# Mixed-head attention with two feed-forward layers: v in seven DMAs by key, weight DMAs on two queues, another listed order

## The chip, the cores and the metric

One core of a Trainium2 chip runs the whole program. The metric is the device time of one execution in microseconds. The kernel before has a median of 1281.13 us in 3 runs (1278.77 to 1286.63). The profiled execution took 1281.71 us, with a span of 1280.0 us from its first to its last instruction.

## The reference, cut to what matters

Four batches of 12 heads, 448 positions, head size 64, all float32. The scores of all heads are mixed by a 12x12 matrix before the softmax, and the attention weights by another one after it:

```python
scores = scale * np.matmul(q, k.transpose(0, 1, 3, 2))
scores = np.einsum('bhij,hg->bgij', scores, w_pre)
attn = exp(scores - max); attn = attn / (sum + 1e-09)
attn = np.einsum('bhij,hg->bgij', attn, w_post)
x = np.matmul(attn, v)                       # then to [1792 tokens, 768]
x = (1 / (1 + exp(-(x @ w_gate))) * (x @ w_val)) @ w_out     # d_ff 1536
h = x @ w_in; out = (h * (1 / (1 + exp(-1.702 * h)))) @ w_out2   # d_ff 2048
```

## The kernel before

**Stages.** Attention comes first, about the first 388 us of the span, and the two feed-forward layers fill the rest. In attention, queries go in 16 units (4 a batch, 120 queries or 88 in the last). For each unit TensorE forms the scores of the six head pairs (`qk`, L343), the scores are copied to SBUF (`sc`), and the SP queue's DMAs rearrange them (`relayout`, L362, tile `gt`), so that one partition holds one query of one head. The units are cut into 92 groups. For each group, in order: two relayouts, `premix` (TensorE, L371), `rowmax` (VectorE, L377), `expo` (ScalarE, L383), `norm` in three steps (ScalarE L391, VectorE L393, GpSimd L396, which makes the tile `w`), `postmix` (TensorE, L418), and copies to the tile `at` (L306). When a unit's groups are done, `av` (TensorE, L439) multiplies `at` with the tile `vt` of its batch, the result is copied to `xo`, and `store` (L456) writes it to DRAM.

**Buffers that couple these.** There are five `gt` buffers, one `at`, one `vt`, one `pf` and two `pc`. So v of a batch can be loaded only after the last `av` of the batch before it, and the first `av` of its own batch waits for it.

**v before.** `load_v` (L325, the DMA at L329) fills `vt`. Key 7m+g of a head stands in partition m + 64*(g // 4) and column g % 4. The kernel before loads it in 8 DMAs a batch, each for three heads and for g = 0 to 3 or g = 4 to 6. A run of 4 or 3 neighbouring keys is one packet of 1024 or 768 bytes. Each DMA writes 64 partitions.

**Weights during attention.** `prepare` (L928) takes 28 blocks of the first layer's weights through attention: a DMA brings a block of 384 KB into `pf` (L938, packets of 1024 bytes), ScalarE (L896, L897) and VectorE (L899, L900, L902) change its number format into `pc`, and a DMA writes 192 KB to the DRAM tensor `kept` (L904). All of these DMAs are issued by SP.

**The order.** Each such step is a numbered piece, given to `work.add` with its needs, the buffers that it takes and gives, the engines that may run it and durations that were used to plan. `PLAN` is a written list of all pieces in the order in which they are emitted. A token is the piece's number in base 36, a letter for the engine where it is not the first one allowed (S ScalarE, V VectorE, P GpSimd, Y SP), and after a colon the PSUM banks. `order()` (L45) reads the list and chooses nothing. Every engine and every DMA queue works through its own pieces in this order, and a piece whose semaphore is not there yet holds up all behind it on that engine or queue.

Of the kernel before, what the change touches and what calls it, by code (L numbers as in the profile page):

```python
# [9 lines left out]
F32 = mybir.dt.float32  # L10
# [69 lines left out]
32 33 3a:34 3b 4q 4r 3p 3r 3d 5dV 2s:62 2tS 3c 3e 40:57 2uS 5cS 34 35:60 41 3f 3s 3g 42 3h 43 44 4d:34 4e 4f  # L80
4g 3i:21 3jS 4h 36V 37S 4i 3kV 45 4j 82:57 88:36 89V 8b:21 46 8aS 83S 3t 8e:40 8cV 84V 8gV 85:63 87V 1gl 86S
8fS 4k 47 8h:52 1gm 4s 8dS 4t 4u 48:76 4l:04 4mS 8jS 49V 4aS 4nS 4v dt:3 duV 5n 5o 3u 60 61 6d 6e 6q 6r 73
3v:17 3wS 1gn 3xS 5p:02 5q 62:64 8iS 5s 4w:1 4x 6f:75 dz 6g 74 5r 5t 5u 6i 5v 7g 7h 8k 8l 1go 4y 50:0 51 6h 52
6j 63 65 dv 1g5 6s:27 64 6t 66 67 68 6k 5w 6v 4zS 6u 5x:56 5yS 75:34 5zV 76 69 6a:12 6bV 8x 8y 6l 6m 1gq e0
az:56 78 6w 77 b1S 53V 6x 6y 7i:73 6n:16 7j 79 7l 8m:04 6oV 6cS 9a 9b b0S 7k 7m 7n 6z 6pV 7a 9n 70:25 7o 9o
71S 72S ds 7p 7b 7c b8:71 ef 8n 8o b9V b5:36 b2:25 1gr b7V b3S b4S a0 1gp 8p e1:7 1gs e2S 7q:06 baV 8q en e3
8r e7 1gt 7d:21 7rS 1gu 7eS 9c:54 7fV 7sS 8z:70 b6V 9d 9f 9p:26 9q 90 9s 9e 9g 9r 1gw a1 91 9t e4:1 e5V dw:3
dxS 7t:5 7u 7v 7wS be:42 bgS 8s 54P bb:76 bdV 1gx dy 1gy qe eh:5 eiS 92 ej 93 ad ae 8t e6 1g6 1gz 1h0 ep:2 eqS
er 7x:6 e8 9u 9h 9i 9j qm 7y eg 7z 80S qf 94 bcS 1h2 a2:35 a3 bfS a5 eo 8u:01 af:62 ag e9:7 qg:4 a4 8vS 8wS a6
qhS 9v 1gv eaV ai ec:3 edV qo:0 eb a7 a8 ee ah bh bi aj ak 9k:15 9lS ek:6 9mV ev:72 ewS ey:31 exS f0S qi bu bv  # L90
c7 elV f1:54 f2S a9 qpV qj:7 al am 1h1 qkS 9w c8 ezS f3V qq ql es:2 etS aa:15 abS eu 1h3 1h4 an:40 aoS 9x:37
95 96 fa:21 9yS 9zS ck cl qu em acV apS f7:46 f9S fbS f8S 1h5 1h6 fcS f4:35 f6V bj:70 f5V bk bm bw:62 bx bl cx
bz 97:54 bn 98V 99S cy 1h8 c9:31 ca cc cm:70 cb bo aq:4 ar as by cn au:5 c0 av aw cd 1g7 cp atS c1 81P ce bp
bq cz:36 cf co c2 1h9 1ha cq fd cr cs 1hb 1hc c3 axS d0 cg fe fq fr g3 g4 gg br:21 bsS d2 ff:47 fg 1h7 ct d1
d3 btV gh fh gt 1he ch:05 ciV cjS fi cu:23 cvV i0:61 i9:40 iaV cwS fj ayP d4 gu ibS i6:53 i7V d5 fk fl i3:27
h6 h7 if:40 i8S i1S ic:35 idV ieV i4S i2S ihS fs:62 ft i5S g5:10 fv gi:73 1hd qv g6 igS fu fw fx c4:45 fy d6
d7:62 c5V c6S d8V d9S gv:54 gw 1hf gx gy fm qn da:2 db dc de:6 df gz g7 1hg g8 g9 ga ii h0 ij iv gj gl gk gm
1hh 1hi gn gb dg fn:54 foV gc iw j8 j9 jl jm ddV fz h8:10 h9 qr:7 hb h1 h2 fpS 1hk qsV 1g8 g0:34 dhS ik:52 il
ha in qt g1S g2S hj hc go gp gd:61 im io kx:34 geV hk kyS l9:05 laV lbV 1hl h3:72 h4S kzV hl hm hn ho hp l6:63
hq hd ip l7V l8S l3:05 l5S l4S 1hm 1hn he hf 1ho gfS lc:74 l0:36 ldV jy l2S h5S jz gq:50 l1S jn:16 1hj kb grV  # L100
ix:72 iy iq gsS hg:35 hhV ir j0 leS hiS ja:04 iz j1 j2 j3 jb jo jq jc 1hq kc ra lf hr:5 jd lg ls je hs ht huS
hv:3 hw hx 1hp hyV 1hr jp 1hs k0:72 is:04 lt m5 k1 jr k3 jf itV kd:53 m6 1g9 k2 mi iuV k4 139 j4 ke nu:16 nvV
k5 js nx:70 nwS jg jh k6 kg 1ht j5:24 kf rc:6 mj kh ki nyV nzS 1hu qw:1 ri rdS j6S jt qxV kj qy ji:53 jjV 1hw
jkS r2 j7S lh:70 ju li lk lj ll lu:21 lv lx kk lw jv:35 rb o6:47 ly o8S qz:0 k7 re r0S r1 mk:26 ml jwS r3 mn
# [54 lines left out]
def attention(tc, q, k, v, w_pre, w_post, xd, after):  # L159
# [7 lines left out]
    nc = tc.nc  # L167
    B, H, S, D = q.shape
# [37 lines left out]
    nu = len(units) // B  # L206
# [1573 lines left out]
```

## Time and profile before

| what | value |
|---|---|
| median of 3 runs | 1281.13 us |
| profiled execution, its span | 1281.71 us, 1280.0 us |
| PE, DVE, ACT, POOL busy | 97%, 78%, 64%, 5% of the span |
| PE instructions | 12770 matmuls, 12770 weight loads |
| DMA packets | 215855, of them 60028 under 512 bytes |
| HBM read, written | 160.18 MB, 55.97 MB |

Busy shares are averages over the two stages, which differ: attention has 8,000 of the matmuls in about 388 us, most of them small. The queue SPq is SP's; its DMAs have a row when they are issued, and the time that a row shows is that of the issue. PE's "issue" as a releaser is idle time in which PE waited for nothing that the profile shows. The granted clock of PE is 1.00 for 2.4 GHz and 0.50 for 1.2 GHz. DMA share is the mean busy share of the 16 DMA engines; as packets of several queues overlap, it can pass 1.

### The profile page before, as it was taken

How to read it: one execution, taken by the hardware profiler on the slowest of the kernel's cores; microseconds unless marked ns; L12 is line 12 of the kernel's file. 1: busy time of each engine (PE TensorE's matmuls, PEld its weight loads, DVE VectorE, ACT ScalarE, POOL GpSimd, SP SyncE). 2: the span in 40 equal slices, each digit the busy share in tenths (PEclk: the TensorE clock that was granted, in tenths of full speed). 3: DMA queues.
4: the chain of work that ended last, by engine and by line, in shares of the span. 5: the costliest groups of instructions: out<-in, count | busy, mean ns of one | idle time of the engine just before them, and what ended most of it. 6: DMA issues, size and time to landing. Idle time of an engine off the chain costs nothing.

```text
span 1280.0 us, 33240 instructions
## 1 busy us (share of the span) xinstructions
PE 1243.6 (97%) x12770; PEld 1112.2 (87%) x12770; DVE 998.1 (78%) x2134; ACT 822.6 (64%) x1976; POOL 58.5 (5%) x139
## 2 busy tenths in 40 slices
PE   7999998899989999999999999999999999999998
PEld 4677676687779899989999999999999989999998
DVE  5687787888877999898799888779756795565763
ACT  3788787888764776776567666556655555565432
POOL 3111111111100000000000000000000000000000
PEclk9999999999999999999999999999999999999999
DMA  6777878778667654589875545885526872125643
GB/s 163 219 203 232 217 217 239 202 236 232 224 217 240 211 180 149 166 294 330 306 270 185 165 157 195 275 287 193 178 77 195 277 256 81 54 68 159 211 147 124
DMA packets 215855, 256.88 MB, mean 201 GB/s; under 512 B 60028, under 2 KB 202160, under 8 KB 215696
## 3 DMA queue, kind: packets, MB, share of 16 engines
q1 hardware_dynamic: 208992, 248.97, 61.6%
q0 software_dynamic: 1488, 4.51, 1.2%
q8 instruction: 101, 1.65, 0.5%
q10 hardware_dynamic: 5216, 1.26, 0.5%
q14 instruction: 58, 0.48, 0.1%
HBM read 160.18 MB, written 55.97 MB: 169 GB/s over the span
## 4 chain that ended last, share of the span: by engine, by line
PE 49%; DVE 7%; DMA 6%; ACT 2%; issue 2%; SPq 0%; DVEq 0%; ACTq 0%
PE pq L1161 27%; PE po L1648 16%; PE py L1106 6%; DMA ws<-in_moe_w_in_dram 3%; DMA sb<-xy 2%; DVE w L1028 1%; DVE xy L1143 1%; DVE s L1299 1%; DVE wc L900 1%; ACT ws L897 1%; ACT xy L1142 1%; DVE wc L902 1%; DVE s L1170 1%; DMA xy<-kept 0%; ACT w L1022 0%
## 5 line engine op out<-in xcount | busy, mean ns | idle before, releaser
L1161 PE MATMUL pq<-xy,w 128*128 128x448 f32 x2394 | 482.3, 362 | 1.8 <-ACT s L1210 0.9
L1161 PEld LDWEIGHTS pq<-xy,w 128*128 128x128 f32 x2394 | 447.7, 187 | 35.8 <-ACT s L1210 2.4
L1648 PE MATMUL po<-wf,xy 128*128 128x384 f32 x1176 | 206.9, 337 | 2.6 <-ACT xy L1094 1.6
L1648 PEld LDWEIGHTS po<-wf,xy 128*128 128x128 f32 x1176 | 206.1, 188 | 3.3 <-ACT xy L1094 1.9
L1106 PE MATMUL py<-xy,w 128*128 128x448 f32 x864 | 173.7, 362 | 1.4 <-DVE xy L1092 1.4
L1106 PEld LDWEIGHTS py<-xy,w 128*128 128x128 f32 x864 | 161.9, 187 | 12.9 <-DVE xy L1092 2.1
L383 ACT ACTIVATE ex<-bank,st 128x448 f32<-128x448 f32 x184 | 116.0, 638 | 23.9 <-DVE st L377 23.7
L418 PEld LDWEIGHTS bank<-w,ex 60*64 60x64 f32 (+1 forms) x5152 | 100.2, 134 | 34.9 <-issue 26.6
L1142 ACT CAST xy<-xy 128x384 fp32r<-128x384 f32 (+2 forms) x212 | 89.3, 457 | 58.2 <-DVE xy L1299 55.1
L377 DVE TENSOR_REDUCE st<-bank 128x1 f32<-128x448 f32 x184 | 106.4, 614 | 21.2 <-PE bank L371 20.9
L418 PE MATMUL bank<-w,ex 60*64 60x60 f32 (+2 forms) x5152 | 104.1, 220 | 9.8 <-issue 8.8
L1143 DVE TENSOR_TENSOR xy<-xy 128x384 fp32r<-128x384 f32 (+2 forms) x212 | 95.5, 483 | 23.1 <-ACT xy L1142 22.7
L1299 DVE TENSOR_TENSOR xy<-xy 128x384 f32<-128x384 f32 (+2 forms) x184 | 90.7, 510 | 14.8 <-DMA xy<-kept 7.2
L371 PE MATMUL bank<-gt,wpre 64*64 64x448 f32 (+2 forms) x736 | 95.1, 552 | 1.8 <-DMA gt<-sc 1.2
L1022 ACT CAST w<-xy 128x384 fp32r<-128x384 f32 x110 | 55.2, 510 | 51.8 <-DVE xy L1299 30.9
L439 PEld LDWEIGHTS bank<-at,vt 128*64 128x64 f32 x1536 | 73.9, 137 | 14.0 <-ACT at L306 5.4
L896 ACT ACTIVATE wc<-ws 128x384 f32<-128x384 f32 x108 | 59.8, 554 | 35.2 <-DMA ws<-in_moe_w_in_dram 24.8
L439 PE MATMUL bank<-at,vt 128*64 128x120 f32 (+1 forms) x1536 | 78.7, 261 | 2.4 <-issue 1.3
L1028 DVE TENSOR_TENSOR w<-wt,w 128x384 fp32r<-128x384 f32 x108 | 59.1, 552 | 26.9 <-ACT w L1022 26.9
L343 PE MATMUL bank<-kq 64*120 64x448 f32 (+1 forms) x576 | 73.9, 393 | 2.8 <-issue 1.8
L306 ACT COPY sc<-bank 120x448 f32<-120x448 f32 (+1 forms) x121 | 59.4, 546 | 19.0 <-DMA nat<-in_q_dram 9.0
L1170 DVE TENSOR_TENSOR s<-s,pq 128x448 f32<-128x448 f32 x80 | 49.2, 616 | 28.5 <-PE pq L1161 28.4
(98 smaller groups left out, 1524.0 us busy)
## 6 DMA issues: line engine op xcount, KB each, us to landing
gt<-sc SPq DMA_DIRECT2D x160, 210.0 KB
wf<-sb SPq DMA_DIRECT2D x64, 384.0 KB
xy<-kept SPq DMA_DIRECT2D x60, 384.0 KB
ws<-in_moe_w_out_dram SPq DMA_DIRECT2D x56, 384.0 KB
kept<-wc SPq DMA_DIRECT2D x108, 192.0 KB
ws<-kept SPq DMA_DIRECT2D x46, 384.0 KB
sb<-xy SPq DMA_DIRECT2D x32, 384.0 KB
ws<-in_moe_w_in_dram SPq DMA_DIRECT2D x32, 384.0 KB
```

The lines of the kernel that those rows point to most:

```text
L343: nc.tensor.matmul(ps[a][:n, :S], w[at_, qp, 1, i0:i0 + n], w[at_, kp, 0], start=(i == 0), stop=(i == 2), tile_position=(a * 64, 0))
L371: nc.tensor.matmul(pre[s][row][64 * col:64 * col + 64, :S], wpre[r], x[r, col], start=True, stop=True, tile_position=(64 * row, 64 * col))
L377: nc.vector.tensor_reduce(out=rs[s][:, j:j + 1], in_=pre[s][j][:, :S], axis=AX.X, op=ALU.max, negate=True)
L383: nc.scalar.activation(ex[s][:, j], pre[s][j][:, :S], AF.Exp, bias=st[:, j:j + 1], scale=1.0, accum_out=st[:, 2 + j:3 + j])
L418: nc.tensor.matmul(ps[row][64 * k:64 * k + 64, c, :, j * m:(j + 1) * m], e[r, j, (c + k * NC) * 64:(c + k * NC + 1) * 64], w[r, j, :, i0:i ...
L439: nc.tensor.matmul(psv[u, half][a * 64:a * 64 + 64, r, :n], vt[:, g, c, :], at[:, c, g, :n], start=(c == 0), stop=(c == NC - 1), tile_posi ...
L1106: self.nc.tensor.matmul(acc[hb][:, :self.S], st, act[k0 + kc][hb][:, ap], start=(k0 + kc == 0 and part == 0 and ap == 0), stop=(k0 + kc == ...
L1142: self.nc.scalar.copy(dst[:, 0], src)
L1143: self.after(n, lambda: self.nc.vector.tensor_tensor(out=dst[:, 1], in0=src, in1=dst[:, 0].bitcast(F32), op=ALU.subtract))
L1161: nc.tensor.matmul(x, st, A[p][c][:, ap], start=(first and c + part + ap == 0), stop=(c == self.KG - 1 and part == 1), skip_group_check=no ...
L1299: self.nc.vector.tensor_tensor(out=dst, in0=x, in1=y, op=op)
L1648: nc.tensor.matmul(acc[:, :PW], x[:, part], w[:, wp], start=(start and part == 0 and wp == 0), stop=(stop and part == 1), skip_group_check ...
```

## The change

v of a batch comes in seven DMAs, one for each g: all 12 heads, every seventh key, 64 partitions, 768 packets of one row of v (256 bytes), 192 KB. The two DMAs of a weight block (into `pf` and to `kept`) may be issued by SP or by GpSimd; the list says which. The pieces are 2134 where they were 2138. The list is a new one; its tokens can't be compared one by one, so this table counts what it says:

| the list | before | after |
|---|---|---|
| `pf` loads on SP, on POOL | 28, 0 | 10, 18 |
| `kept` stores on SP, on POOL | 28, 0 | 7, 21 |
| `xd` stores on SP, on POOL | 3, 13 | 0, 16 |
| DMAs on POOL in all (without the set-up) | 13 | 55 |
| second relayout of a group to its `premix`: mean distance in the list, least, under 10 tokens | 42.8, 1, 8 groups | 49.4, 7, 1 group |
| `norm` on POOL directly behind a DMA on POOL | 11 | 34 |
| `norm` on POOL to its `postmix`: mean distance, 2 tokens or fewer | 21.6, 5 groups | 19.6, 17 groups |
| of the groups with 2 tokens or fewer: `norm` directly behind a POOL DMA at most 12 tokens before | 0 | 5 |
| load of a block to its first use on ScalarE: mean distance, least | 25.4, 1 | SP 24.4, 7; POOL 35.4, 14 |
| batch 0, SP's order behind the 12 relayouts of groups 0 to 5 | a pair of `nat` DMAs, a `pf` load, six v DMAs, relayout 6 | five v DMAs, relayout 6 |

ScalarE copies 9 pieces fewer of `sc` and `at` and 10 more of `kq` and `xo`; VectorE the reverse. PE has the same pieces, with nearly the same order of kinds: 94 changes of kind before, 92 after, among `qk`, `premix` with `postmix`, and `av`.

```diff
-    VH = 3
...
-        def load_v(b, x, h0):
-
-            c = slice(x * NC, min(x * NC + NC, HC))
-            h = slice(h0, h0 + VH)
-            nc.sync.dma_start(vt[64 * x:64 * x + 64, h, :c.stop - c.start],
-                              v[b, h].rearrange("h (m g) d -> m h g d", g=HC)[:, :, c])
+        def load_v(b, g):
+
+            x, c = divmod(g, NC)
+            nc.sync.dma_start(vt[64 * x:64 * x + 64, :, c], v[b].rearrange("h (m g) d -> m h g d", g=HC)[:, :, g])
...
-                    for c in range(2):
-                        for h0 in range(0, H, VH):
-                            vready[b].append(work.add((first[u] + 2 + 2 * c) * STEP + 1113 + 300 * h0, dict(SP=(650, 850)),
-                                                      load=(2650, 2070)[c] * VH // H,
...
+                    for g in range(HC):
+                        vready[b].append(work.add((first[u] + 2 + 0.5 * g) * STEP + 1113, dict(SP=(650, 850)), load=4720 // HC,
+                                                  emit=lambda e, b=b, g=g: load_v(b, g), takes=() if vready[b] else ("v",),
...
-                self.nc.sync.dma_start(st.rearrange("p (k f) e -> p k (f e)", k=nk), src)
+                (e or self.nc.sync).dma_start(st.rearrange("p (k f) e -> p k (f e)", k=nk), src)
...
-                tiles["f"][j]()
+                    tiles["c"] = c
+                if j == 4:
+                    (e or self.nc.sync).dma_start(self.kept[i // 2][i % 2], tiles["c"].bitcast(F32))
+                else:
+                    tiles["f"][j]()
...
-            x = work.add(t, dict(SP=(540, 1800)), load, takes=("pf",), since=t, load=1300)
+            x = work.add(t, dict(SP=(540, 1800), POOL=(900, 2400)), load, takes=("pf",), since=t, load=1300)
...
-                                         dict(DVE=(470, 575)), dict(SP=(500, 900)))):
+                                         dict(DVE=(470, 575)), dict(SP=(500, 900), POOL=(800, 1300)))):
```

## Rows read from the trace of the kernel before

**Rows 1.** Windows: three stretches, busy us of PE, PEld, DVE, ACT, POOL, clock, DMA share, GB/s
```profile
0.00:32.00 32.00, 23.19 (x128) 15.29 (x132) 19.17 (x48) 9.69 (x20) 12.14 (x34) 1.00 0.68 163
32.00:388.00 356.00, 338.01 (x8109) 262.11 (x8102) 280.87 (x604) 285.20 (x791) 45.56 (x104) 0.99 0.76 221
388.00:1280.00 892.00, 882.41 (x4538) 834.75 (x4537) 698.05 (x1484) 527.74 (x1168) 0.79 (x1) 1.00 0.59 194
```

**Rows 2.** Timeline of PE: start, us, operation, count, idle time before it and releaser
```profile
44.43 0.45 PE L418 MATMUL bank<-w,ex 60*64 60x60 f32 x9 [2.35 <-issue]
...
139.38 2.30 PE L343 MATMUL bank<-kq 64*120 64x448 f32 x19 [1.79 <-issue]
...
213.16 0.86 PE L418 MATMUL bank<-w,ex 48*64 48x48 f32 x42 [1.62 <-issue]
...
219.25 0.99 PE L439 MATMUL bank<-at,vt 128*64 128x88 f32 x21 [1.33 <-issue]
...
231.44 0.73 PE L418 MATMUL bank<-w,ex 60*64 60x60 f32 x29 [2.64 <-issue]
...
373.51 3.15 PE L1106 MATMUL pg<-xy,w 128*128 128x448 f32 x8 [2.46 <-issue]
```

**Rows 3.** Windows: two stretches at a lower granted clock
```profile
45.90:49.10 3.20, 3.20 (x22) 2.73 (x20) 2.18 (x7) 2.70 (x9) 1.12 (x3) 0.50 0.65 245
...
373.00:377.00 4.00, 3.49 (x28) 2.71 (x31) 0.81 (x2) 0.68 (x2) 0.00 (x0) 0.57 0.32 96
```

**Rows 4.** Page, part 3: the queue of kind instruction, packets, MB, share
```profile
q8 instruction: 101, 1.65, 0.5%
```

**Rows 5.** Timeline of SP's queue: start, us of issue, DMAs in a row
```profile
23.90 10.36 SPq L362 DMA_DIRECT2D gt<-sc  x12
34.32 1.23 SPq L293 DMA_DIRECT2D nat<-in_k_dram  x2
35.59 0.58 SPq L938 DMA_DIRECT2D pf<-in_moe_w_gate_dram  x1
36.22 3.98 SPq L329 DMA_DIRECT2D vt<-in_v_dram  x6
40.60 8.94 SPq L362 DMA_DIRECT2D gt<-sc  x9
...
130.68 7.22 SPq L329 DMA_DIRECT2D vt<-in_v_dram  x8
...
305.45 7.61 SPq L329 DMA_DIRECT2D vt<-in_v_dram  x8
```

**Rows 6.** Windows: q and k arriving (2 to 9), v arriving, a weight block arriving (220.8)
```profile
2.00:9.00 7.00, 3.39 (x16) 2.73 (x16) 3.36 (x8) 1.63 (x2) 5.41 (x8) 1.00 1.08 221
40.00:44.00 4.00, 1.44 (x55) 0.79 (x48) 2.31 (x5) 2.49 (x9) 0.39 (x1) 1.00 1.08 180
...
222.00:232.00 10.00, 6.90 (x241) 5.30 (x233) 6.83 (x16) 6.91 (x20) 1.85 (x4) 1.00 1.07 176
307.00:315.00 8.00, 7.68 (x263) 6.57 (x259) 7.09 (x18) 6.96 (x20) 1.52 (x5) 1.00 1.11 205
...
220.80:222.00 1.20, 1.20 (x32) 0.84 (x32) 0.31 (x1) 0.92 (x2) 0.00 (x0) 1.00 1.07 339
```

**Rows 7.** Waits of PE, 32 to 384 us: who for whom, us, times, longest
```profile
PEld bank L418 <- POOL w L396: 4.5, 10, 1.4
...
PEld bank L371 <- DMA gt<-sc: 3.4, 5, 1.3
...
PE bank L371 <- DMA gt<-sc: 0.7, 2, 0.5
```

**Rows 8.** Waits of SP's queue to 384 us
```profile
SPq L938 <- DVE pc L902: 24.5, 14, 5.3
```

**Rows 9.** Tile xo: issue ns least, median, most; and time to landing
```profile
L456 POOL DMA_DIRECT2D xd<-xo x13: 787/803/869, 70.7 to 389.5; - x13
...
DMA to landing us min/median/max: 3.9/5.7/7.4
```

More of the change, by code (lines that the diff above doesn't have):

```diff
@@ L80 @@
[L80 to L104, printed above, removed]
@@ L150 @@
[L150 to L154 removed]
+0Y 1S 3:0 2Y 6:1 9:2 4V 5 7V cS 10S 8 f:3 1cY 1f:4 gV 1dS h 11Y 13:5 16:6 1gV 1i:7 oS pY aV dS 1oS 14V 1h
@@ new lines @@
+3s 4d:60 37S 4e 4g 3i:27 3jV 3kV 81:35 83V 45 8d:41 46 dq 4f 4h 4i 5n 4j 4k 3t 82S 87:26 84:70 89S 8g:53 47 5z
+88V 85S 8iS 8eS 8fV 86S 8a:26 8bS 4l:71 4mS 60 4nS 8cS 3u 3v:34 3wV 48:02 49S 4aV 8hS 5o:71 3xV 1ggP 61:63
+ds:0 5p 4v:2 5r 5q 5s 62 5t dtS du 63 5u 6c 6d 6p 6q 72 1gh 4w 4x 6e:54 64 1gi 5v 65 4z:7 50 51 73 6f 6r:16
+1gj 66 7f 4yS 7g 1g1 8j 8k 5w:03 6h 6g 1gk 6i 6s 6j 52S 6u 6t 6v 74:25 75 dy ay:47 6k 1gmP 8w 8x 99 6w 6x
+7h:16 9a 9m 9n 5xS azS 77 67 6y b0S 6l 76 78 5yV 79 68 7i 7k 7j 7l 7m 6z:04 70V 71V ee 7a 69:73 7b 6m:25 6nS
@@ new lines @@
+iv:13 lbV jw r8 l3S lcV 1hmP he jl:74 hf:65 hgV ip hhS jx k9 j8:02 jm j9 ja iw jn hp:5 hq jo iy hr ht:6 jp jb
+jc jd hu ka ld le lq lr m3 m4 hsV 1hn 1ho 1hp jq hv ix iz jy:07 r0 jz j0 k1 jr js hwS iq:45 irS k0 k2 1g5 j1
+kb:21 k3 isV ns:36 mg nv:45 nxS je kc jf 136 1hq ke kd jg:07 jhS jiV ra:5 rbV j2 ntV nuS nwS rc mh qu:2 qvS
+dhP rg 13e kf kg j3:07 lf:64 lg 1hsP j4S j5S li ls:35 jt:10 mt mu kh k4 k5 qw lh qx:7 lj lt juS ki lv o4:62
+o5V o6V qyV 1hlP lu lw kj:41 jvS kkS mi:35 1hrP lk r9 klS mj mk ml m5:60 m6 qz k6:24 k7V o7:13 mm r1 o9V k8S
@@ new lines @@
+1ht o1:57 o2S 1hu ny:42 1hv 1hw o3V n6 n7 nzS mn m8 o0V lx km:3 kn m7 ko o8S m9 kq:5 kr kpV ll r2:4 ly r3V r4
+mo ma ri:6 rjS mb 138:7 rd:1 reS rf rh 139S r5:2 1hyY 13a 13g:0 r6S r7 oa ob rk ks n8:34 lz 13hS on 13i 1hz
+1i0 1i1 lm ln:17 137 mp 1i2 1g6 ktS 1hxP m0:26 n9 loS lpS nb m1S m2S mv:05 mw my mq:17 na nc mx mz mrV msV
+rl:2 nd rmV ne oo rn p0 p1 13b:6 n0 1i4Y n1 pd 13cV 13d ro:34 rpS s0:10 13u rqS s2S rx:75 ryV 1i3P pe s3:32
+rzS mc ru:40 rr:56 s5S nf rvV s4S pq pr 1g7 1i5 1i6 1i7 13f 1i8 md:27 oc:34 rtS rsS n2 1iaY s1V meS mfS rwS s6
@@ L155 @@
+1ek 1fl 1fm 1m6 1deV 1f9 1l6 1li 1fn 1ge 1e8:01 1m7 1lj 1lk 1e9S 1l9 1eaS 1m8 1m9 1ey:32 1l8 1ezS 1f0V 1mb 1lo
+1fo:01 1el:32 1ll 1lc 1mc 1lm 1md 1lp 1la 1my 1emS 1ln 1lq 1mz 1fa 1ls 1enV 1fb:32 1lw 1me 1lr 1fpS 1fqS 1lt
+1n0 1mf 1le 1mg 1lu 1fcV 1lv 1fdS 1lx 1fr:0 1fs 1lg 1ft 1m0 1m1 1mi 1mj 1n1 1ly 1lz 1m4 1m5 1m2 1m3 1aiP 1lb
+1mk 1n2 1n3 1dfP 1fv:1 1fw 1ml 1mm 1mn 1mp 1mq 1n4 1n5 1n6 1ld 1lf 1lh 1mr 1mh 1ms 1mt 1mu 1mw 1mx 1ma 1fuS
+1fx 1fyS 1fz 1mv 1n7 1n8 1mo 1n9
 """
@@ L601, in attention @@
                     vready[b] = []
-                    for c in range(2):
-                        for h0 in range(0, H, VH):
-                            vready[b].append(work.add((first[u] + 2 + 2 * c) * STEP + 1113 + 300 * h0, dict(SP=(650, 850)),
-                                                      load=(2650, 2070)[c] * VH // H,
-                                                      emit=lambda e, b=b, c=c, h0=h0: load_v(b, c, h0), takes=() if vready[b] else ("v",),
-                                                      behind=vready[b][-1:], since=0 if b else THIRD))
+                    for g in range(HC):
+                        vready[b].append(work.add((first[u] + 2 + 0.5 * g) * STEP + 1113, dict(SP=(650, 850)), load=4720 // HC,
+                                                  emit=lambda e, b=b, g=g: load_v(b, g), takes=() if vready[b] else ("v",),
+                                                  behind=vready[b][-1:], since=0 if b else THIRD))
                 add_av(u)
@@ L944, in step @@
                     tiles["f"] = self.convert(i, tiles["st"], c)
-                tiles["f"][j]()
-            x = work.add(t, dict(SP=(540, 1800)), load, takes=("pf",), since=t, load=1300)
+                    tiles["c"] = c
[4 more added lines that the diff above has]
+            x = work.add(t, dict(SP=(540, 1800), POOL=(900, 2400)), load, takes=("pf",), since=t, load=1300)
             for j, engines in enumerate((dict(ACT=(890, 1010)), dict(DVE=(270, 385)), dict(DVE=(470, 590)),
-                                         dict(DVE=(470, 575)), dict(SP=(500, 900)))):
-                x = work.add(t + j + 1, engines, lambda e, j=j, step=step: step(e, j), needs=[x], load=670 if j == 4 else 0,
+                                         dict(DVE=(470, 575)), dict(SP=(500, 900), POOL=(800, 1300)))):
+                x = work.add(t + j + 1, engines, lambda e, j=j, step=step: step(e if j == 4 else None, j), needs=[x], load=670 if j == 4 else 0,
                              takes=("pc",) if j == 0 else (), gives=((), (), (), ("pf",), ("pc",))[j])
```

115 lines of the change are left out of this document (60 added, 55 removed).

## Prediction

> **What bounds the kernel now.** I read the windows by stage first. From 388 us on, PE stands idle 892.00 - 882.41 = 9.6 us [rows 1], and nothing of the change runs there. I take that stage as unchanged. In the 388 us of attention PE is idle 8.8 us in the fill and 18.0 us behind it, while DVE and ACT are busy 79% and 80% [rows 1]. So PE sets the pace there, with little room: all its idle time is 26.8 us, 2.1% of the span. The timeline of PE comes next: six gaps make 2.35 + 1.79 + 1.62 + 1.33 + 2.64 + 2.46 = 12.2 us of it [rows 2]. The reader is to see two things. All six are put down to "issue", so no engine and no DMA in the profile released them. And three of them (44, 139 and 231 us) end in or just behind the time in which v arrives [rows 5, 6]. Two gaps cost twice: after those at 44 and 373 us the granted clock is at the lower level, 0.50 for 3.2 us and 0.57 on average over 4 us [rows 3]. Half of 3.2 us, and 0.43 of 4 us, are 1.6 and 1.7 us of lost PE work. My best reading of the six gaps is PE's own instructions arriving late: attention holds 64% of the matmuls in 30% of the span [rows 1], and the instruction queue brings 1.65 MB in 101 packets, 16.3 KB each [rows 4]. The profile does not name it as their releaser, so it stays a reading.
>
> The Trainium skill, "Runtime: NRT & Kernel Launch", section on instruction fetch mechanics, says that blocks of 16 KiB are fetched ahead and that this is mostly hidden. The block size agrees with 16.3 KB [rows 4]; if the hiding held here, the six gaps would need another cause.
>
> **Step 1, v's DMAs.** 32 issues become 28 and the bytes stay. SP is held 3.98 us by six, 7.22 and 7.61 us by eight, 0.66 to 0.95 us each [rows 5], and it is held at the pace of the transfer: a batch of 1.376 MB at 176 to 205 GB/s is 7.8 to 6.7 us [rows 6]. Packets fall to 256 bytes, 5376 a batch for 1536. No row shows 256-byte packets into 64 partitions, so I bound them. The nearest row is that of q and k, 256-byte packets from the same memory into 112 partitions: 221 GB/s is 863 packets a us, at share 1.08 and 16 engines 20 ns a packet. That gives 5376 x 20 / 16 = 6.7 us, the low end. For the high end: a v packet now takes 16 x 1.07 / (176 / 0.896) = 87 ns, a weight packet of about that size, into 128 partitions, 52 ns (339 GB/s) [rows 6]. The 35 ns more are what the 64 partitions cost. A quarter of them on a quarter of the bytes makes 29 ns, 9.7 us a batch. So -1 to +3 us a batch against 7.2 to 7.6 today. I take 0, by the nearer row (size, source and queue are the same); the ends are -4 and +12 us of SP's time in all, of which the list hides a part.
>
> The Trainium skill, "DMA: Bandwidth & Descriptors", section Specifications, gives 512 bytes as the least transfer for line rate, which speaks against this step. The trace agrees in part: 221 GB/s in small packets against 339 in large ones [rows 6], but v's large packets ran at only 176 to 205. By that rule v would take longer than today (rival C), by the nearer row it does not.
>
> **Step 2, batch 0's v.** Behind the twelve relayouts SP now issues a pair, a `pf` load and six v DMAs, and relayout 6 goes out at 40.60, 6.3 us after the twelve ended [rows 5]. PE, ACT and DVE then ran dry until 44.43 [rows 2]. After the change five v DMAs stand there, 5 x 0.66 to 0.95 = 3.3 to 4.8 us, so relayout 6 goes out 1.6 to 3.0 us earlier. If the gap of 2.35 us and its 1.6 us of clock hang on relayouts and saturated DMA there, up to 4 us go; if they are instructions alone, none. I take -2.5 us, nearer the upper end, because the work that the relayout feeds also comes earlier.
>
> **Step 3, relayouts ahead.** PE waits 3.4 + 0.7 = 4.1 us for `gt` [rows 7]. Eight groups have their second relayout fewer than 10 tokens ahead of `premix` before, one after. A token is 356 / 2134 = 0.17 us on average, so the mean lead grows from 7.1 to 8.2 us. That can take away 0 to 4 us; I take -1.5, since part of the waits are behind slow DMA and not behind a late place in the list.
>
> **Step 4, weights on POOL.** 39 issues leave SP, and three stores besides. SP now waits 24.5 us at 14 of 28 `pf` loads for DVE to free the buffer [rows 8], with relayouts queued behind; 18 of 28 of this, 15.8 us, moves to POOL, where the `norm` of the next groups queues behind, and behind that `postmix` on PE. POOL has room in sum: an issue there takes 0.80 us [rows 9], 42 more are 34 us on 58 us of busy time. But 34 norms follow directly on a POOL DMA where 11 did, and 17 groups where there were 5 have `postmix` at most two tokens behind. Of those, 5 have both. Five times 0.80 us is 4 us at most where the list is right about DVE, nothing where PE is busy with another group. PE waits for `w` 4.5 us today [rows 7]. I take +0.5 us, near the low end, as PE was rarely kept (10 times) with 11 such norms. A load lands later: 5.7 us for a POOL DMA [rows 9], and the list leaves 14 tokens or 2.3 us in the tightest place, 35 tokens or 5.9 us on average; ACT, at 80%, takes that slack.
>
> The Trainium skill, "SBUF — State Buffer", section on the two separate sides, says that while VectorE holds the port it shares with GpSimd, GpSimd cannot write descriptors for its DMAs, so they wait. Today's 13 issues show none of it, 787 to 869 ns [rows 9]; by the rule, landing would spread, and rival B would gain.
>
> **Step 5, the rest of the order.** The other four gaps depend on where a burst of small matmuls meets a busy stretch of DMA. DMA stays as loaded (0.76 [rows 1]), with the same pieces on PE. I take 0; the ends are all gone, -8.2 us and 1.7 us of clock, or as many new ones, +8.
>
> **Sum.** 0 - 2.5 - 1.5 + 0.5 + 0 = -3.5 us. The profiled execution took 1281.71 us, 0.6 above the median and within the runs' spread. So 1278.2 us, with 1274 to 1282 as this case's own range. About 1%, 12.8 us, is what a measurement can tell from no change here.
>
> **Rivals.**
> - A, the gaps go. The new order keeps bursts away from v and weights, and all six gaps with both clock losses vanish: -12.2 - 3.3 = -15.5, with step 3 some 1266 us. For it: lists and queues both changed at three gaps. Against: v saturates DMA as before. Chance 0.13.
> - B, POOL's queue becomes the wait (slower than before). A `pf` load at POOL's head waits for DVE, 24.5 / 14 = 1.75 us on average, and issues 0.80 us; a norm behind it is 2.55 us late. It decides where the norm's lead over `postmix` (19.6 tokens, 3.3 us on average, two tokens for 17 groups) is shorter. Five groups have both by the list; if twice as many do on the chip, 10 x 2.55 = 25 us, less overlap with other PE work by half: +12, so 1278.2 + 12 = 1290. Chance 0.12.
> - C, small packets are dear. At 9.7 us a batch the three batches whose v phase already cost PE lose 2.5 us more each: 1278.2 + 7.5 = 1286. If the 35 ns fall on every packet whatever its size, 55 ns and 18.5 us a batch, 11 us late against a lead of 8: 3 more for each of four batches, near 1298. The rule of the Trainium skill cited in step 1 points this way. Chance 0.10.
> - D, the change is off the path: gaps stay in other places, 1281.7 within 1.5. Chance 0.15.
>
> **The numbers.** The forecast has 0.50. Faster by over 1% (under 1268.3): 0.10 of A and 0.02 of the rest. Slower by over 1% (over 1293.9): 0.03 each of B and C. Within 1%: 0.82. The range from 1267 to 1290 leaves out half of A and the dear halves of B and C, under 2 in 10.
>
> **What would show it.** Step 1: v phases of 7 us at a share near 1 and about 190 GB/s; under 150 GB/s it is C. Step 2: relayout 6 issued before 39.5 us, and no stretch at half clock before 60 us. Step 3: PE's waits for `gt` under 3 us. Step 4: PE's waits for `w` near 5 us; over 12 us it is B. Step 5: four to seven gaps over 1 us, put down to "issue". The feed-forward stage must stay at 892 us within 2; if it moves, the premise that only attention changes is wrong.

## The result, and the profile after

The changed kernel took 1291.11 us (median of 10 runs, 1285.11 to 1296.18) against 1280.05 us for the kernel before, run beside it (10 runs, 1273.85 to 1286.63). The ratio is 1.009 with a 95% interval of 1.0064 to 1.0115, so it is slower by 11 us. Ratios, here and below, leave out the few executions that took over 1.5% longer than the fastest of their kernel (one of e14_best took 2032.76 us); medians are of all. The prediction was 1278.2 us in a range of 1267 to 1290: the sign was wrong, and the time lies outside the range. Its profiled execution took 1291.4 us, with a span of 1289.7 us.

Windows of the kernel before, cut where VectorE starts the first gate product of the feed-forward stage (396.50 us); columns as in [rows 1]:

```profile
0.00:396.50 396.50, 369.70 (x8276) 285.36 (x8277) 304.28 (x660) 298.60 (x815) 58.48 (x139) 0.99 0.76 218
```

The same of the changed kernel, cut at the same instruction (405.90 us), with the stretch behind it and the middle one of [rows 1]:

```profile
0.00:405.90 405.90, 371.94 (x8273) 287.40 (x8274) 306.25 (x657) 299.10 (x818) 88.77 (x181) 0.98 0.79 213
405.90:1289.70 883.80, 874.23 (x4499) 827.50 (x4497) 693.55 (x1476) 524.82 (x1161) 0.00 (x0) 1.00 0.59 193
32.00:388.00 356.00, 329.46 (x7959) 255.75 (x7960) 274.41 (x586) 275.68 (x765) 75.82 (x146) 0.98 0.81 219
```

The difference of the two profiled executions, 9.7 us, lies in attention: it ends 9.4 us later. The rest takes 883.8 us where it took 1280.0 - 396.5 = 883.5. Of the 9.4 us, 34.0 - 26.8 = 7.2 are idle time of PE, and 2.2 are more busy time for the same matmuls, at a lower mean clock (0.98 for 0.99).

PE's gaps of over 1 us in attention, behind the fill, to be held against [rows 2] (the line numbers are one to four lower after the change):

```profile
50.95 0.97 PE L369 MATMUL bank<-gt,wpre 64*64 64x448 f32 x4 [1.06 <-DMA gt<-sc]
...
138.94 2.97 PE L341 MATMUL bank<-kq 64*120 64x448 f32 x14 [4.15 <-issue]
...
147.56 0.50 PE L416 MATMUL bank<-w,ex 60*64 60x60 f32 x14 [1.16 <-issue]
...
229.53 0.69 PE L416 MATMUL bank<-w,ex 60*64 60x60 f32 x23 [2.87 <-issue]
...
248.77 0.68 PE L416 MATMUL bank<-w,ex 60*64 60x60 f32 x23 [1.88 <-issue]
...
319.03 3.03 PE L416 MATMUL bank<-w,ex 60*64 60x60 f32 x92 [2.15 <-issue]
...
330.77 4.73 PE L437 MATMUL bank<-at,vt 128*64 128x120 f32 x88 [1.45 <-DMA vt<-in_v_dram]
...
379.24 3.11 PE L416 MATMUL bank<-w,ex 60*64 60x48 f32 x117 [2.63 <-issue]
```

They make 17.4 us where the six of before made 12.2. The gap at 44 us is gone. Those at 139 and 230 us, in the v phases, are longer, and there is one at 319 us, in that of batch 3. SP's v DMAs (start, us of issue), against [rows 5]:

```profile
21.11 10.40 SPq L360 DMA_DIRECT2D gt<-sc  x12
31.57 7.43 SPq L328 DMA_DIRECT2D vt<-in_v_dram  x5
39.12 0.97 SPq L360 DMA_DIRECT2D gt<-sc  x1
...
125.47 1.85 SPq L328 DMA_DIRECT2D vt<-in_v_dram  x2
129.15 9.20 SPq L328 DMA_DIRECT2D vt<-in_v_dram  x5
...
218.60 7.34 SPq L328 DMA_DIRECT2D vt<-in_v_dram  x5
227.23 1.87 SPq L328 DMA_DIRECT2D vt<-in_v_dram  x2
...
310.89 8.02 SPq L328 DMA_DIRECT2D vt<-in_v_dram  x5
320.16 1.31 SPq L328 DMA_DIRECT2D vt<-in_v_dram  x2
```

The reader is to see five DMAs that hold SP as long as eight did, or longer. Windows of the v phases of batches 1 and 2 (against [rows 6]) and of the stretch at a lower clock behind the longest gap (against [rows 3]):

```profile
130.00:140.00 10.00, 5.85 (x140) 5.12 (x138) 6.57 (x15) 5.10 (x14) 1.85 (x4) 0.89 1.05 156
136.00:144.00 8.00, 5.06 (x74) 4.04 (x78) 1.82 (x5) 2.10 (x5) 1.54 (x3) 0.62 1.07 156
219.00:229.00 10.00, 7.66 (x239) 5.67 (x235) 7.68 (x19) 7.65 (x23) 1.16 (x4) 1.00 1.16 185
```

Waits of PE and of ScalarE from 32 to 384 us (who for whom, us, times, longest), against [rows 7]:

```profile
PEld bank L416 <- POOL w L394: 3.4, 9, 0.8
PEld bank L369 <- DMA gt<-sc: 4.8, 5, 1.8
PE bank L369 <- DMA gt<-sc: 1.6, 3, 1.1
PEld bank L437 <- DMA vt<-in_v_dram: 2.5, 2, 1.7
PE bank L437 <- DMA vt<-in_v_dram: 2.0, 2, 1.4
ACT pc L892 <- DMA pf<-in_moe_w_val_dram: 6.9, 8, 1.7
ACT pc L892 <- DMA pf<-in_moe_w_gate_dram: 1.2, 1, 1.2
```

PE's wait for `w` fell from 4.5 us, its wait for `gt` rose from 4.1 to 6.4 (weight loads and matmuls added up, as in step 3; the matmuls' part is 1.6, and was 0.7), and a wait for v is new. The weight loads on POOL and their landing (issue ns least, median, most), against [rows 9]:

```profile
L934 POOL DMA_DIRECT2D pf<-in_moe_w_gate_dram x9: 759/805/845, 43.2 to 332.7; - x9
L934 POOL DMA_DIRECT2D pf<-in_moe_w_val_dram x9: 792/805/811, 71.9 to 346.5; - x9
...
DMA to landing us min/median/max: 4.2/6.8/8.4
```

### The profile page after: what moved, and what is told of

It is laid out like the page before. It is cut to its first block, busy times and chain, and to the rows that moved or that the text cites. A ratio compares the mean times of both kernels' runs of the same rounds, so it can differ in the third digit from the quotient of the medians.

```text
span 1289.7 us, 33238 instructions
## 1 busy us (share of the span) xinstructions
PE 1246.2 (97%) x12770; PEld 1114.9 (86%) x12770; DVE 999.8 (78%) x2131; ACT 823.9 (64%) x1979; POOL 88.8 (7%) x181
## 4 chain that ended last, share of the span: by engine, by line
PE 56%; DVE 5%; issue 1%; DMA 1%; ACT 1%; DVEq 0%; ACTq 0%
PE pq L1161 28%; PE po L1648 16%; PE py L1106 13%; DVE w L1028 1%; DVE xy L1143 1%; DVE s L1299 1%; DVE wc L896 1%; DMA sb<-xy 1%; DVE s L1170 0%; DMA wf<-sb 0%; ACT xy L1142 0%; DVE xy L1299 0%; DVE wt L1299 0%; DVE wc L895 0%; DVE wc L898 0%
## 5 line engine op out<-in xcount | busy, mean ns | idle before, releaser
L375 DVE TENSOR_REDUCE st<-bank 128x1 f32<-128x448 f32 x184 | 107.0, 615 | 26.1 <-PE bank L369 25.4
L369 PE MATMUL bank<-gt,wpre 64*64 64x448 f32 x736 | 95.2, 556 | 2.6 <-DMA gt<-sc 1.6
L1170 DVE TENSOR_TENSOR s<-s,pq 128x448 f32<-128x448 f32 x80 | 49.4, 618 | 28.4 <-PE pq L1161 28.4
L341 PEld LDWEIGHTS bank<-kq 64*120 64x120 f32 (+1 forms) x576 | 52.6, 181 | 20.0 <-issue 5.7
```

The costliest lines, as they stand in the source:

```text
L341: nc.tensor.matmul(ps[a][:n, :S], w[at_, qp, 1, i0:i0 + n], w[at_, kp, 0], start=(i == 0), stop=(i == 2), tile_position=(a * 64, 0))
L369: nc.tensor.matmul(pre[s][row][64 * col:64 * col + 64, :S], wpre[r], x[r, col], start=True, stop=True, tile_position=(64 * row, 64 * col))
L375: nc.vector.tensor_reduce(out=rs[s][:, j:j + 1], in_=pre[s][j][:, :S], axis=AX.X, op=ALU.max, negate=True)
```

## The experiments

"Large" below is v in seven DMAs of 192 KB with packets of 1024 or 768 bytes, "small" v as the change has it. Each ratio is against the kernel before in runs beside it, with its 95% interval. A row's difference to another row is worth less than a row by itself, since each has its own interval: taken as independent, the two leave it uncertain by 0.4 to 0.5%. A trace is of one execution, and those of one kernel differ: e3_list's twelve lie from 1272.8 to 1293.5 us, six of them over 1289, the traced one at 1274.9.

| kernel | list | v | weights on POOL | median, us | ratio |
|---|---|---|---|---|---|
| changed | new | small | loads, stores | 1291.11 | 1.009 [1.0064, 1.0115] |
| e1_large | new | large | loads, stores | 1290.71 | 1.0077 [1.0046, 1.0108] |
| e2_sp | new | small | none | 1286.0 | 1.0048 [1.0014, 1.0082] |
| e3_list | new | large | none | 1284.98 | 1.0028 [0.9992, 1.0065] |
| e10_keeps_pool | new | large | stores | 1284.4 | 1.0019 [0.9989, 1.0049] |
| e11_loads_pool | new | large | loads | 1293.56 | 1.010 [1.0073, 1.0127] |
| e13_early_loads | new, loads earlier | large | loads, stores | 1296.59 | 1.011 [1.0057, 1.0163] |
| e12_list_inter | new | large, halves in turn | none | 1276.3 | 0.9962 [0.9935, 0.9989] |
| e5_small_inter | new | small, halves in turn | loads, stores | 1285.77 | 1.0043 [1.0017, 1.0068] |
| e4_before_small | old | small | none | 1283.21 | 1.0035 [1.001, 1.0059] |
| e9_before_pool | old | large | loads, stores | 1303.26 | 1.017 [1.0139, 1.0202] |
| e15_old_loads | old | large | loads | 1302.32 | 1.019 [1.0139, 1.024] |
| e16_old_keeps | old | large | stores | 1282.25 | 1.0025 [0.9996, 1.0055] |
| e8_no_v | old | batch 0 alone | none | 1268.43 | 0.9899 [0.9869, 0.9928] |
| e7_before_inter | old | large, halves in turn | none | 1273.07 | 0.9931 [0.9906, 0.9956] |
| e14_best | old | large, halves in turn | stores | 1275.81 | 0.9972 [0.9943, 1.0] |

### The change taken apart in the new list

e1_large puts v back into large packets, at the same places of the list:

```diff
-            x, c = divmod(g, NC)
-            nc.sync.dma_start(vt[64 * x:64 * x + 64, :, c], ...)
+            x, n = divmod(g, NC)
+            h = slice(4 * n, 4 * n + 4) if x else slice(3 * n, 3 * n + 3)
+            c = slice(x * NC, min(x * NC + NC, HC))
+            nc.sync.dma_start(vt[64 * x:64 * x + 64, h, :c.stop - c.start], ...)
```

> The changed kernel with v again in packets of 1024 and 768 bytes: seven DMAs of 192 KB in the same seven places of the same list (four of three heads and g = 0 to 3, three of four heads and g = 4 to 6). Theory S (small packets make each v phase some 3 us longer, and PE's gaps there with it): most of the 11 us come back, 1279 to 1284 us, v phases of about 7 us, no gap over 3 us. Theory P (weight DMAs on POOL) and theory L (the order of the list is worse by itself): stays at 1288 to 1292 us.

e2_sp puts the weights' DMAs back on SP. e3_list does both, so that the new order is left (with seven v DMAs for eight, three more `xd` stores on POOL, and some copies on the other engine):

```diff
-                (e or self.nc.sync).dma_start(st..., src)
+                self.nc.sync.dma_start(st..., src)
...
-                    (e or self.nc.sync).dma_start(self.kept[i // 2][i % 2], ...)
+                    self.nc.sync.dma_start(self.kept[i // 2][i % 2], ...)
```

> The changed kernel with all 28 weight loads and 28 kept stores issued by SP, in the same places of the list; v stays in small packets. Theory P: 5 us or more come back, 1280 to 1286 us. Theory S: no gain, 1289 to 1295 us, as SP also has to issue 39 DMAs more. Theory L: no change within 3 us of 1291.

> The changed kernel's list alone: v in large packets in seven DMAs, all weight DMAs on SP. Theory S: 1278 to 1285 us, as the kernel before. Theory L: 1286 us or more although neither of the two other parts of the change is left. Theory P: below the run with large packets and weights on POOL by 5 us or more.

e10_keeps_pool and e11_loads_pool are e1_large with one of these two lines put back.

> The new list with v in large packets, the 28 weight loads on SP and only the 21 kept stores on POOL. Beside it stand the same list with both on POOL (0.8% over the kernel before) and with both on SP (0.3% over). Theory L1 (the loads are what costs on POOL: they land 6 us after their issue and ScalarE, in order, waits for them): as with both on SP, 1280 to 1284 us beside 1279. Theory Q (any DMA on POOL's queue costs, by slots on the engines or by norms behind it): half of the difference, 1283 to 1287.

> The new list with v in large packets, 18 weight loads on POOL and all kept stores on SP. Theory L1: as with both on POOL, 1287 to 1291 us beside 1279. Theory Q: half of the difference, 1283 to 1287.

The four kernels on the new list give the terms. POOL's part is 1.009 - 1.0048 = 0.42% with small packets and 1.0077 - 1.0028 = 0.49% with large ones: 5 to 6 us of 1280, each about as large as its uncertainty. The small packets are 0.13% (changed less e1_large) and 0.20% (e2_sp less e3_list), some 2 us, and within it. The order alone is +0.28%, 3.6 us, with an interval that just holds zero (-1.0 to +8.3 us). That the three add up to the result is no test, since each is a step from one row to the next; what is tested is that a part costs about the same with and without the other. Of POOL's part the stores cost nothing that can be seen (1.0019, against 1.0028 without them), and the loads all of it: the intervals of e10_keeps_pool and e11_loads_pool don't touch. e11_loads_pool has only five runs, four of 1291.6 to 1296.5 us and one, the profiled one, of 1276.7; the old list has to bear it out.

### The parts in the old list

e4_before_small gives the kernel before the small packets, in seven of its eight places a batch. e9_before_pool issues the same 18 loads and 21 stores on POOL that the new list does, at their old places; e15_old_loads moves the loads alone, e16_old_keeps the stores alone:

```diff
+            g = NC * x + h0 // VH
+            if g < HC:
+                nc.sync.dma_start(vt[64 * x:64 * x + 64, :, g - NC * x], ...)
```

```diff
-                self.nc.sync.dma_start(st..., src)
+                queue = self.nc.gpsimd if i in self.PL else self.nc.sync
+                queue.dma_start(st..., src)
...
+                if j == 4 and i in self.PK:
+                    self.nc.gpsimd.dma_start(self.kept[i // 2][i % 2], ...)
```

> The kernel before, its own list, with v in small packets alone (seven DMAs in the first seven of the eight places, the eighth place empty). Theory S: slower by 6 to 12 us, 1286 to 1292 us, with larger gaps of PE at 40, 135 and 225 us. Theories P and L: 1278 to 1283 us, as before.

> The kernel before, its own list and v in large packets, with the same 18 weight loads and 21 kept stores on POOL that the change puts there. In the two pairs on the new list the weights on POOL cost 0.42 and 0.49%, 5 to 6 us. Theory P (POOL's queue costs by itself, whatever the list): 1283 to 1287 us beside 1279. Theory P2 (it costs only in the new list, which puts norm and postmix close behind those DMAs): within 2 us of the kernel before. In both, if norms are what is late, PE's waits for w grow from 4.5 us to 8 or more; if PE's instructions are what is late, they stay and the idle time put down to issue grows.

> The kernel before with only the 18 weight loads on POOL. Theory L1 (a load on POOL lands later than the list allows, ScalarE waits in order, and all behind it): nearly all of the 1.7%, 1298 to 1305 us beside 1281, ScalarE's waits for pf over 20 us where the kernel before has 4. Theory Q (each DMA on POOL's queue costs alike): 18 of 39 parts, 1289 to 1293.

> The kernel before with only the 21 kept stores on POOL. Theory L1: no change, 1279 to 1284 us beside 1281, as nothing in attention waits for them but the next use of one of two buffers. Theory Q: 21 of 39 parts, 1291 to 1295.

Here too the loads carry it: 1.9%, four times what POOL costs on the new list, and more than either theory gave e9_before_pool. The stores are 0.25%, with an interval that just holds zero, and e4_before_small's 1283.21 us lies at the edge of what theories P and L gave it, short of theory S. e15_old_loads also shows how, in this list. Its waits from 32 to 384 us:

```profile
ACT pc L898 <- DMA pf<-in_moe_w_val_dram: 21.3, 6, 6.9
PEld bank L418 <- POOL w L396: 5.2, 11, 1.4
```

The kernel before has 3.0 us in the first of these rows:

```profile
ACT pc L896 <- DMA pf<-in_moe_w_val_dram: 3.0, 4, 1.0
```

So it is ScalarE that stands, and PE's wait for `w` is what it was [rows 7]. One such place, from its timelines of VectorE, POOL, ScalarE and PE:

```profile
313.22 0.56 DVE L904 SCALAR_TENSOR_TENSOR pc<-pf,pc 128x384 uint32<-128x384 uint32 x1
...
316.05 0.39 POOL L396 TENSOR_TENSOR w<-wpost,st 128x120 f32<-128x120 f32 x1 [8.62 <-DVE st L393]
316.51 0.80 POOL L941 DMA_DIRECT2D pf<-in_moe_w_val_dram  x1
...
324.85 0.54 ACT L898 ACTIVATE pc<-pf 128x384 f32<-128x384 f32 x1 [4.01 <-DMA pf<-in_moe_w_val_dram]
...
325.75 1.37 ACT L306 COPY sc<-bank 120x448 f32<-120x448 f32 x3
326.31 1.85 PE L418 MATMUL bank<-w,ex 60*64 60x60 f32 x53 [3.93 <-ACT sc L306]
```

VectorE's last step on the block before frees `pf` at 313.22 + 0.56 = 313.78 us. A norm on POOL waits 8.62 us for VectorE, and the load behind it on POOL goes out when the norm is done, at 316.51, 2.7 us after it could have. It lands 324.85 - 316.51 = 8.3 us later, beside v's DMAs (SP is held by them from 309.47 to 317.65). ScalarE, which has the conversion of this block next in its order, stands for 4.01 us; the copies of scores behind it are late, and PE stands for 3.93. SP, which issues loads in the kernel before, had no norms in its queue; there the load of this block went out at 304.89, 0.08 us after `pf` was free.

The other places are like it. Of the 17 loads on POOL behind the first, seven go out 2.6 to 7.0 us after `pf` was free, each with a norm that had waited directly ahead of it, and five of these seven are followed by 22.0 of the 23.4 us that ScalarE waits for `pf` in all (21.3 and, for the other matrix, 2.1).

The changed kernel, in its traced execution (1291.4 us, at its median), does not lose its time in this way. Of its 17 loads behind the first, 15 go out 0.53 to 0.59 us after `pf` was free, the other two 0.96 and 1.55; mostly POOL already stands idle at the load when the buffer comes free. One of them, from its timelines of VectorE and POOL (the buffer is free at 332.09):

```profile
331.53 0.56 DVE L898 SCALAR_TENSOR_TENSOR pc<-pf,pc 128x384 uint32<-128x384 uint32 x1
...
332.66 0.81 POOL L934 DMA_DIRECT2D pf<-in_moe_w_gate_dram  x1 [3.87 <-ACT ex L381]
```

### Loads earlier in the new list

In e13_early_loads, POOL's 17 later loads of e1_large stand directly behind the last conversion step of the block before; 16 of them move, by 16 tokens on average (an edit of the list alone).

> The new list with large packets and both weight DMAs on POOL, where the 17 POOL loads behind the first stand directly behind the step that frees their buffer, 16 tokens (2.7 us) earlier on average. It stood at 0.8% over the kernel before, with the weights on SP at 0.3%. Theory L1: 0.3 to 0.5%, 1284 to 1287 us beside 1280. Theory N (norms queue behind the DMAs on POOL): no better or worse, 1290 or more, as POOL now waits for VectorE in front of more norms.

It is not faster than e1_large, and it could not bring a load forward: in e1_large too, 15 of the 17 go out 0.53 to 0.59 us after `pf` was free, and there is one `pf`. ScalarE's waits for `pf` stay at 6.1 us in both. But POOL now stands at the loads with more norms behind them. PE's waits for `w` in e13_early_loads:

```profile
PEld bank L339 <- POOL w L317: 8.9, 11, 2.4
```

The same in e1_large:

```profile
PEld bank L419 <- POOL w L397: 4.2, 8, 1.2
```

By which of its waits the changed kernel loses its 5 to 6 us on POOL is not settled: ScalarE waits for `pf` 8.1 us there (6.9 + 1.2), but 7.2 us in e10_keeps_pool too, which has its loads on SP, and the profiled executions of e1_large and e11_loads_pool (1277.7 and 1276.7 us) lie 13 and 17 us under these kernels' medians, so their traces don't show the loss.

### What v costs

e8_no_v leaves out v of batches 1 to 3 (`if b: return` ahead of the DMA in the kernel before).

> The kernel before without the loads of v of batches 1 to 3 (v of batch 0 is used for all, so 24 DMAs and 4.1 MB are left out). Theory S (a v phase saturates the DMA engines and PE's gaps there follow from it): PE's gaps at 139 and 231 us go, 4 to 8 us less in all, 1271 to 1275 us. Rival (the gaps are where PE's stream of small matmuls is dense, whatever the DMA does): the gaps stay, 1277 to 1280 us.

These three v phases cost 1.0%, 13 us, more than theory S gave them. Windows from 120 to 240 us, where two of them lie, first of the kernel before:

```profile
120.00:240.00 120.00, 110.53 (x2723) 84.87 (x2717) 94.61 (x203) 92.15 (x256) 15.06 (x33) 1.00 0.81 219
```

and of e8_no_v:

```profile
120.00:240.00 120.00, 118.62 (x2939) 92.12 (x2930) 100.86 (x219) 98.67 (x278) 16.60 (x37) 1.00 0.71 213
```

PE's idle time falls from 9.5 to 1.4 us, and the largest gap left in it is 0.63 us. That looks as if the gaps put down to "issue" at 139, 213, 219 and 231 us [rows 2] hung on v's DMAs, but two of them end before v of batch 2 is issued (219.51), and e16_old_keeps, with v loaded as before (from 129.78 and 219.23), has neither of the other two (e9_before_pool and e15_old_loads have both). Its windows:

```profile
120.00:240.00 120.00, 114.56 (x2729) 89.21 (x2724) 94.96 (x206) 92.38 (x257) 20.43 (x44) 0.97 0.78 220
128.00:144.00 16.00, 16.00 (x464) 12.73 (x464) 11.87 (x29) 13.15 (x38) 2.63 (x6) 1.00 0.85 207
```

With v loaded in the old list, then, PE's idle time in these 120 us is 5.4 us here, 6.4 in e4_before_small and 3.7 in e7_before_inter. So the time shows that v's loads cost; what makes the gaps is not shown, nor that the DMAs hold up PE's instructions.

m1_v_alone issues only v loads, one batch after another, each phase behind a copy on VectorE that waits for all of the phase before; nothing else of the reference is computed. "mix" is one DMA of each half of the partitions in turn, "wide" is other rows of v, as many bytes, into all 128 partitions with each DMA (in the large form six DMAs for eight).

> Only loads of v, a batch at a time with a wait between, in six forms; nothing of the reference is computed. Large packets as before, small ones as after, both again with the two halves of the partitions in turn, and both into 128 partitions with the same rows. Theory H (small packets and half of the partitions add up): large 6 to 7 us, small 10 to 11 us, small in turn and small into 128 partitions 6 to 7 us, large into 128 partitions 4 us. Theory S (a cost of each small packet whatever the partitions): all three small forms 10 us, all three large ones 5 to 7 us. The forecast's own reading (q and k's row): small as large, 6.7 us.

Its timeline, the DMAs of a phase and the copy that waited for it:

```profile
19.60 5.77 SPq L32 DMA_DIRECT2D small<-in_v_dram  x7
30.04 0.22 DVE L52 COPY bigmix<-small 128x42 f32<-128x42 f32 x1 [10.47 <-DMA small<-in_v_dram]
...
38.63 0.21 DVE L52 COPY smallmix<-bigmix 128x42 f32<-128x42 f32 x1 [8.16 <-DMA bigmix<-in_v_dram]
...
48.35 0.21 DVE L52 COPY smallwide<-smallmix 128x42 f32<-128x42 f32 x1 [9.29 <-DMA smallmix<-in_v_dram]
...
57.00 0.21 DVE L52 COPY bigwide<-smallwide 128x42 f32<-128x42 f32 x1 [8.23 <-DMA smallwide<-in_v_dram]
...
64.27 0.21 DVE L52 COPY big<-bigwide 128x42 f32<-128x42 f32 x1 [6.85 <-DMA bigwide<-in_v_dram]
64.51 5.22 SPq L27 DMA_DIRECT2D big<-in_v_dram  x8
...
73.61 0.21 DVE L52 COPY small<-big 128x42 f32<-128x42 f32 x1 [8.91 <-DMA big<-in_v_dram]
```

From the first issue to the copy a batch takes 73.61 - 64.51 = 9.1 us large and 30.04 - 19.60 = 10.4 us small (9.8 in a second phase). Halves in turn take 8.35 and 9.3 us (from 30.28 and 39.08), all partitions 7.0 and 8.4 us (from 57.24 and 48.59). Small packets cost about a microsecond a batch (0.7 to 1.4); writing one half of the partitions after the other costs 1.4 to 2.1 us beside all of them. These are single phases of one execution, and the form that came twice differed by 0.6. Theory H had the order of the forms right, but not its sizes: the halves in turn give back only a part of what all partitions do.

That points to a version of v that is cheap to make. e7_before_inter is the kernel before with its eight DMAs a batch in another order, one of each half in turn; e12_list_inter and e5_small_inter do the same in e3_list and in the changed kernel; e14_best is e7_before_inter with 21 stores on POOL:

```diff
         def load_v(b, x, h0):
+            x, h0 = divmod(NC * x + h0 // VH, 2)[::-1]
+            h0 *= VH
```

```diff
         def load_v(b, g):
+            g = (0, 4, 1, 5, 2, 6, 3)[g]
```

> The kernel before with its eight v DMAs of a batch in another order: the two halves of the partitions in turn (0 to 63, 64 to 127, 0 to 63, ...) instead of four and four. Theory H (the 64 partitions of one DMA set v's rate, as my upper bound assumed): v phases shrink from 7 to 5 us or less, 1274 to 1278 us. Rival (v's rows set the rate, whatever the partitions): no change, 1278 to 1281 us.

> The new list, large packets, all weights on SP, and v's seven DMAs with the two halves of the partitions in turn. On the kernel before, taking the halves in turn took 0.7% away. Theory H (two DMAs that write different halves run beside each other): 0.4 to 0.8% below the same kernel with the halves one after the other, 1273 to 1277 us beside 1279. Rival (it was a lucky place in the old list): 1280 to 1285. If it comes out below the kernel before with the halves in turn (0.993), it is the best version.

> The changed kernel as it is, with the seven small-packet DMAs of v in the order g = 0, 4, 1, 5, 2, 6, 3, so that the halves of the partitions alternate. Alone, such loads took 9.3 us against 9.8 to 10.4 in order. Theory H: 3 to 7 us less than the changed kernel, 1284 to 1288 us beside 1279. Theory S (the cost of a small packet does not depend on the partitions): within 2 us of 1291.

> The kernel before with v's eight large DMAs taking the halves of the partitions in turn (0.7% below it) and the 21 kept stores on POOL, which on the new list cost nothing. Theory L1: 1271 to 1275 us beside 1281; SP is freed of 21 issues of 0.5 us, so perhaps 1 to 2 us below the halves in turn alone. Theory Q: 1280 or more.

The order of the halves is worth 0.69% in the old list, 1.0028 - 0.9962 = 0.66% in the new one and 0.47% in the changed kernel. e7_before_inter, at 1273.07 us, is the fastest version that computes the reference: 9 us under the kernel before and 18 under the changed one. Four batches at the 0.75 us of m1_v_alone would be 3 us, and SP is held by v for 6.1 to 6.8 us in batches 1 to 3, not 5 or less; through which waits the rest of the 9 us comes is not shown. Stores on POOL bring it no gain: the 1 to 2 us expected of e14_best did not come, and by the two ratios it is 0.4% slower, about as much as their uncertainty.

## Why the prediction was wrong

- **What is to be explained.** The sum was -3.5 us and the result is +11.1. Of these 14.6 us, about 5 are step 4, about 2 step 1, and 7.6 the order (steps 2, 3 and 5 together). Step 4 is the best shown of them, not the largest.
- **Step 4 failed.** It was taken at +0.5 us and measured 5 to 6 us, as far as can be seen all of it from the loads. The step priced the norms behind POOL's DMAs, and dismissed the loads' later landing because "ACT, at 80%, takes that slack". An engine that works in order has no slack for an instruction that stands at its head: in e15_old_loads ScalarE stands 23.4 us so, where it was 4.0. There the norm ahead of the load, at which the step did not look, waits for VectorE, and the load goes out late. In the changed kernel the loads go out within 0.6 us of `pf` being free in 15 of 17 places, ScalarE waits 8.1 us for them, PE waits for the norms' `w` no longer than before (3.4 us), and by which wait the loads cost 5 to 6 us stays open.
- **Step 1 was mis-sized.** It was taken at 0 from the row of q and k, within -4 to +12 us of SP's time. From batch 0's main part on, v held SP for 26.7 us before (3.98 + 7.22 + 1.42 + 6.49 + 7.61, of which the 1.42 and 6.49 of batch 2 are not in [rows 5]) and 37.0 us after (the rows above, from 31.57 on): +10.3, near the high end. In time that was 4.5 us in the old list, and about 2 in the new one, there not clear of noise. The nearer row has q and k go into 112 partitions; in m1_v_alone small packets took 8.4 us into 128 partitions and 9.8 to 10.4 into one half after the other. The reading behind the high end, that 64 partitions cost a packet time, is what m1_v_alone and the halves in turn bear out. The section Specifications of the Trainium skill's "DMA: Bandwidth & Descriptors", weighed there, had the direction right: 9.1 us large, 9.8 to 10.4 small.
- **Step 2 came out by luck.** Relayout 6 went out at 39.12 us, before 39.5, the gap at 44 us is gone, and the first 8 us with a clock below 1 are those from 136 us. But the five v DMAs ahead of it took 7.43 us and not 3.3 to 4.8, and relayout 6 went out 39.12 - 31.51 = 7.6 us after the twelve had ended, where it was 6.3: it was early because the twelve began at 21.11 instead of 23.90. PE then waited for `gt` instead, 1.06 us at 50.95.
- **Step 3 did not come true.** The leads in the list grew, and PE's waits for `gt` grew as well, to 6.4 us where under 3 were its sign. In other kernels with this list they are 0.8 (e1_large) to 4.7 us (e3_list), so one trace doesn't say what the lead is worth.
- **Step 5 and the order as a whole.** Steps 2, 3 and 5 together are the order alone: -4.0 us predicted, +3.6 measured. Zero is inside the interval, -4.0 is not, so the gain failed to come; what in the order costs, if anything does, was not tested. The count of gaps was as said, but at 139 us the gap is 4.15 us, and 8 us from 136 us on run at a mean clock of 0.62.
- **Premise.** The feed-forward stage was to stay within 2 us; it did within 0.3.
- **Rivals.** B had the right queue, but not the wait: PE's wait for `w` fell to 3.4 us, where over 12 was its sign. Its 12 us for POOL alone were twice what the new list lost, and half of the 24 us of the old list. C had the direction right, but its sign, under 150 GB/s, did not come (156 in batch 1's phase, 185 in batch 2's), and its price of 7.5 us is more than the 2 to 4.5 measured. A and D fell. The chance of 0.82 for "within 1%" covers the 0.9% that came, but the range ended at 1290, since each rival was priced by itself and the sum of three costs was not.

## What to carry to other kernels

A DMA that is moved to another queue waits for what stands ahead of it there: look at the longest wait of that queue's own compute, and then at the engine that has the consumer next in its order, however much room it has on average. Compare the time of each issue with the time at which its buffer came free before calling it late. Where an array fills the partitions in two halves, try issuing the halves in turn; it paid in three kernels here. A bound for a DMA comes from rows with the same packet size and the same partitions; where each row shares only one of the two, take neither as the nearer. And a gap that is gone in one trace is no proof: look for it in the traces of the kernels that should have kept it.

## What was not expected of the hardware

- Order alone, with the same DMAs and the same packets, changed the time of a transfer into two halves of the partitions from 9.1 to 8.35 us by itself, and the kernel by 0.69%.
- PE's gaps behind which the profile sees no releaser don't follow one cause that a trace shows: 9.5 us of idle time in 120 us of the kernel before, 1.4 without v, but also 5.4 in e16_old_keeps with v as before.
- The same DMA on POOL, `xd`, was issued in 787 to 956 ns in the changed kernel (median 836), with 55 DMAs on POOL for 13, where it took 787 to 869 (median 803) [rows 9]; the 18 loads took 759 to 845. So what the prediction feared from VectorE, 78% busy in both, shows in the issue times of `xd` by a tenth of a microsecond at most. The landing of `xd` went from 5.7 to 6.9 us in the median, and how much of that is busier DMA is not shown.
